# Two attention batches instead of one ahead of the layer, on the layer's own PSUM banks and buffers, and a planner that counts changes of the array's shape

## The chip, the cores and the metric

The kernel runs on one core of a Trainium2 chip. The metric is the device time of one execution in microseconds (us), the median of several runs. The core has five engines, each with its own queue that runs in order: TensorE (PE in the profile, with PEld for its weight loads), VectorE (DVE), ScalarE (ACT), GpSimd (POOL) and SyncE (SP). SP does no arithmetic here: it issues every DMA of the kernel.

## The reference

A linear attention over 8 batches of 8 heads, 576 tokens and head size 64, followed by a two-matrix layer with a Gelu over all 4608 tokens:

```python
def phi(x):                                   # (8, 8, 576, 64) -> (8, 8, 576, 256)
    proj = np.einsum('bhsd,df->bhsf', x, w_phi)
    proj = proj - np.max(np.abs(proj), axis=-1, keepdims=True)
    return np.concatenate([np.exp(proj), np.exp(-proj)], axis=-1)

q_p, k_p = phi(q), phi(k)
kv  = np.einsum('bhsf,bhsd->bhfd', k_p, v)
z   = np.sum(k_p, axis=2)
num = np.einsum('bhsf,bhfd->bhsd', q_p, kv)
den = np.einsum('bhsf,bhf->bhs', q_p, z)[..., None] + 1e-06
x   = (num / den).transpose(0, 2, 1, 3).reshape(4608, 512)
h   = x @ w_in                                # (4608, 2048)
g   = 0.5 * h * (1.0 + erf(h / sqrt(2)))
out = g @ w_out                               # (4608, 512)
```

## The kernel before, in words

Attention is done batch by batch. `k_quad(b, g)` takes four of a batch's heads. It loads `kt` and `vt`, and in five units it projects keys on PE (tile `pk`), takes the largest absolute value (`mx`) and subtracts it on DVE, takes two exponentials on ACT (`ek`), and sums keys times values on PE into `kv`, which ACT copies to `kvn`. `q_pair(b, p)` takes two heads and handles the tokens in two halves of 288: it projects queries on PE (`pq`), ACT copies them to `pc`, POOL takes the largest absolute value over the partitions (`mb`), DVE subtracts it from `pc`, ACT takes two exponentials (`ef`), and PE multiplies them with `kvn` (`pn`). ACT copies the result to `xo`, and it goes to device memory as `x_d`. The first two batches (`ND = 2`) get the denominator as a 65th row of `pn`. For the other six DVE weights `ef` (`un`) and POOL sums it over the partitions (`db`). `quotients` turns a half batch's denominators into reciprocals `r_d`.

The layer (`block(j, ...)`) runs over 18 blocks of 256 tokens. A block loads `xr` and `rb` (numerators and reciprocals), and DVE makes `xh` and `xl`, the high and low part of their product. Eight steps follow, each with 24 matmuls into `ph`, a Gelu on ACT (`gh`, and `ph` in place), a subtraction on DVE (`gl`), and 12 matmuls into `po`. The weights come as raw 64-bit words: `split_weight` turns each of 32 pieces into a high and a low float with two ACT and five DVE instructions (tiles `wt_` and `w_`). A piece may start 3.996 us after the one before.

Nothing runs in the order in which it is written. Each step is recorded with an engine, a cost, a rank and its buffers, and a planner (`Plan.order`) walks through a model of the engines and writes each engine's program in the order of its modelled starts. Among the steps of an engine that could start within 0.02 us of the earliest, the one with the lowest rank goes first. The chip then runs these fixed orders, each step waiting for what it needs, so a step that comes late holds up all that stands behind it on its engine.

PSUM is shared out as `pp` (two banks, for `pk` and `pq`), `kv`, `pn`, `ph` (two single banks) and `po` (two banks). Only batch 0 goes ahead of the layer: it does both its `k_quad`s first, then all four pairs of one half, then of the other, and its `pk` tiles take turns on `pp` and `po`. The other seven batches are spread over the layer by their ranks.

Of the kernel before, what the change touches and what calls it, by code (L numbers as in the profile page):

```python
# [58 lines left out]
class Plan:
# [191 lines left out]
def fused_kernel(ctx: ExitStack, tc: tile.TileContext, qT, kT, va, w_st, w_in, w_out, out):  # L251
# [48 lines left out]
    def split_weight(src, nm, rank):  # L300
# [8 lines left out]
        op("act", act(512), lambda: nc.scalar.activation(t().bitcast(F32), high().bitcast(F32), AF.Abs), r=[raw], w=[t], **k)  # L309
# [36 lines left out]

    def k_quad(b, g, kvs, rank):
# [18 lines left out]
        for u, (p, cs) in enumerate(units):  # L366
            n = len(cs)
            mx = sb["mx"]([P, 2, n], F32, f"mx_{nm}_{u}")
            e = [sb["ek"]([P, 2, n, NF], F32, f"ek_{nm}_{u}_{s}") for s in range(2)]
# [11 lines left out]
            for s in (1, 0):  # L381
                op("act", act(256 * n, True), lambda xs=xs, e=e, s=s: nc.scalar.activation(  # L382
                    e[s](), xs(), AF.Exp, scale=1.0 - 2.0 * s), r=[x], w=[e[s]], table="exp", **k())
# [24 lines left out]
    def q_pair(b, p, kvs, rank, halves=(0, 1)):  # L408
# [4 lines left out]
        for half in halves:  # L413
# [7 lines left out]
            op("pe", SW + PAIR_Q, lambda pq=pq, qt=qt: [
                mm(pq()[:, j, :HS], lhsT=wst()[64 * j : 64 * j + 64], rhs=qt()[64 * j : 64 * j + 64], start=True, stop=True) for j in range(2)
            ], r=[qt, wst], w=[pq], also=[pc], **k(1))
            copy("act", act(2 * HS, True), pc, lambda pq=pq: pq()[:, :, :HS], [pq], [pc], **k(1))
# [231 lines left out]
```

## Time and profile before

| | |
|---|---|
| median of 3 runs | 1194.47 us (1192.34 to 1195.37) |
| the profiled execution | 1194.14 us, of which the span from first to last instruction is 1192.4 us |
| PE busy | 1131.1 us, 95% of the span |
| ACT, DVE, POOL busy | 602.6, 496.4 and 318.6 us |
| mean granted TensorE clock | 0.977 of full |

The profiled execution is 0.3 us below the median of the runs, and its span lies 1.7 us below its own time. PE's share of busy time is an average over three stages that look different: a head before the layer's first matmul, a stage in which attention and layer share PE, and an end with the layer alone. The views of single stages say more than the page's totals. One matmul of 32-bit floats in the program counts as two in the trace, so that 1280 `kv` matmuls of the program are the 2560 of the page.

### The profile page before, as it was taken

What the parts mean: (1) busy time and instruction counts of PE and PEld (TensorE: products, weight loads), DVE (VectorE), ACT (ScalarE), POOL (GpSimd) and SP (SyncE); (2) the same over time, 40 slices, a digit from 0 to 9 for tenths busy, and PEclk for the clock granted to TensorE, in tenths of its full rate; (3) what the DMA queues carried; (4) which work ended last, traced back from release to release, by engine and by line L of the source; (5) the groups of instructions that cost most, each with busy time, mean ns of one, the idle gap of its engine ahead of it and who ended that gap; (6) DMA issues with size and microseconds to landing.
All of it is one profiled execution on the core that took longest, in us unless ns stands there. A gap on an engine that the chain in (4) does not pass through costs nothing.

```text
span 1192.4 us, 21799 instructions
## 1 busy us (share of the span) xinstructions
PE 1131.1 (95%) x9096; PEld 926.4 (78%) x9096; DVE 496.4 (42%) x807; ACT 602.6 (51%) x973; POOL 318.6 (27%) x116
## 2 busy tenths in 40 slices
PE   5669999989999999998989999999999999999998
PEld 3437688667887878776868787787899899899897
DVE  5888962375444444445253534434221121121110
ACT  4667866746557656665665654767222122122121
POOL 3110200376355353534152625435200000000000
PEclk8798999999999999998989999999999999999999
DMA  7467511242222222222113131201121111010000
GB/s 253 164 189 225 151 64 51 57 130 63 88 75 76 67 74 73 63 68 73 52 40 97 32 108 28 71 24 57 30 54 32 23 53 33 21 37 18 1 18 18
DMA packets 73939, 84.92 MB, mean 71 GB/s; under 512 B 23968, under 2 KB 60992, under 8 KB 73840
## 3 DMA queue, kind: packets, MB, share of 16 engines
q1 hardware_dynamic: 73840, 83.52, 23.6%
q8 instruction: 71, 1.16, 0.4%
q14 instruction: 28, 0.23, 0.1%
HBM read 64.32 MB, written 19.17 MB: 70 GB/s over the span
## 4 chain that ended last, share of the span: by engine, by line
PE 75%; DVE 8%; DMA 6%; ACT 4%; POOL 3%; issue 2%; SPq 1%; ACTq 0%; DVEq 0%; POOLq 0%
PE po L270 31%; PE ph L270 29%; PE kv L270 6%; PE pn L270 4%; POOL db L460 3%; PE pq L270 3%; PE pk L270 3%; DMA rb<-r_d 1%; DVE un L454 1%; DVE mx L378 1%; ACT ek L382 1%; DMA dc<-d_d 1%; DVE un L457 1%; DMA xr<-x_d 1%; DMA raw_i<-in_w_in_dram 1%
## 5 line engine op out<-in xcount | busy, mean ns | idle before, releaser
L270 PE MATMUL ph<-xh,w_i 128*128 128x256 f32 x2304 | 439.1, 284 | 0.0
L270 PEld LDWEIGHTS ph<-xh,w_i 128*128 128x128 f32 x2304 | 364.8, 190 | 18.2 <-issue 10.4
L270 PE MATMUL po<-w_o,gh 128*128 128x512 f32 x1152 | 370.6, 403 | 1.4 <-ACT ob L288 1.3
L270 PE MATMUL ph<-xl,w_i 128*128 128x256 f32 x1152 | 323.8, 281 | 0.0
L294 DVE TENSOR_TENSOR gl<-ph,gh 128x512 fp32r<-128x512 f32 x144 | 99.2, 689 | 378.5 <-ACT ph L548 366.8
L270 PEld LDWEIGHTS po<-w_o,gh 128*128 128x128 f32 x1152 | 209.5, 190 | 55.1 <-issue 10.9
L270 PE MATMUL po<-w_o,gl 128*128 128x512 f32 x576 | 230.7, 401 | 14.0 <-DVE gl L294 14.0
L425 POOL PARTITION_ALL_REDUCE mb<-pc x64 | 142.8, 2231 | 371.6 <-ACT pc L288 284.4
L270 PEld LDWEIGHTS ph<-xl,w_i 128*128 128x128 f32 x1152 | 218.4, 190 | 3.4
L460 POOL PARTITION_ALL_REDUCE db<-un x48 | 177.3, 3694 | 156.1 <-DVE un L457 152.3
L547 ACT ACTIVATE gh<-ph 128x512 fp32r<-128x512 f32 x144 | 86.1, 598 | 258.3 <-PE ph L270 257.7
L270 PEld LDWEIGHTS po<-w_o,gl 128*128 128x128 f32 x576 | 109.5, 190 | 44.0 <-DVE gl L294 18.8
L270 PEld LDWEIGHTS kv<-vt,ek 128*64 128x64 f32 (+1 forms) x2560 | 89.4, 145 | 44.0 <-ACT ek L382 18.1
L270 PE MATMUL kv<-vt,ek 128*64 128x65 f32 (+1 forms) x2560 | 102.0, 233 | 16.0 <-ACT ek L382 13.4
L270 PE MATMUL pn<-ef,kvn 128*64 128x288 f32 (+1 forms) x512 | 98.4, 426 | 14.1 <-ACT xo L288 11.8
L382 ACT ACTIVATE ek<-pk 128x512 f32<-128x512 f32 (+1 forms) x160 | 80.7, 549 | 54.1 <-DVE pk L294 53.7
L431 ACT ACTIVATE ef<-pc 128x576 f32<-128x576 f32 x128 | 81.0, 678 | 37.2 <-DVE pc L294 36.7
L547 ACT ACT_TABLE_LOAD x60 | 77.0, 1283 | 29.7 <-PE ph L270 28.9
L378 DVE TENSOR_REDUCE mx<-pk 128x4 f32<-128x512 f32 (+1 forms) x80 | 50.5, 632 | 97.4 <-PE pk L270 97.4
L548 ACT ACTIVATE ph<-ph 128x512 f32<-128x512 f32 x144 | 85.3, 593 | 0.0
L294 DVE TENSOR_TENSOR pc<-pc,mb 128x576 f32<-128x576 f32 x64 | 50.1, 783 | 77.1 <-POOL mb L425 77.1
L270 PEld LDWEIGHTS pn<-ef,kvn 128*64 128x64 f32 (+1 forms) x512 | 39.7, 138 | 51.2 <-ACT xo L288 20.4
(41 smaller groups left out, 718.9 us busy)
## 6 DMA issues: line engine op xcount, KB each, us to landing
vt<-in_va_dram SPq DMA_DIRECT2D x16, 585.0 KB
qt<-in_qT_dram SPq DMA_DIRECT2D x64, 144.0 KB
kt<-in_kT_dram SPq DMA_DIRECT2D x16, 576.0 KB
out_dram<-ob SPq DMA_DIRECT2D x36, 256.0 KB
raw_i<-in_w_in_dram SPq DMA_DIRECT2D x16, 512.0 KB
raw_o<-in_w_out_dram SPq DMA_DIRECT2D x16, 512.0 KB
x_d<-xo SPq DMA_DIRECT2D x48, 144.0 KB
x_d<-xo SPq DMA_DIRECT2D x32, 72.0 KB
```

The lines of the kernel that those rows point to most:

```text
L270: return tc.keep_in_program_order(nc.tensor.matmul(*a, **kw))
L294: op(eng, cost, lambda: e.tensor_tensor(out=dst(), in0=a(), in1=b(), op=o), r=r, w=w, **kw)
L378: op("dve", dve(256 * n, True), lambda xs=xs, mx=mx: nc.vector.tensor_reduce(out=mx(), in_=xs(), axis=AX.X, op=ALU.max, apply_absolute_val ...
L382: op("act", act(256 * n, True), lambda xs=xs, e=e, s=s: nc.scalar.activation(e[s](), xs(), AF.Exp, scale=1.0 - 2.0 * s), r=[x], w=[e[s]], ...
L425: op("pool", 2.2, lambda mb=mb, pc=pc: nc.gpsimd.partition_all_reduce(mb(), pc(), P, bass_isa.ReduceOp.absmax), r=[pc], w=[mb], **k(1))
L431: op("act", act(2 * HS), lambda ef=ef, pc=pc, s=s: nc.scalar.activation(ef()[:, s], pc(), AF.Exp, scale=1.0 - 2.0 * s), r=[pc], w=[ef], ta ...
L454: op("dve", dve(HS, fast=True) + 0.06, lambda un=un, ef=ef, one=one, j=j: nc.vector.tensor_scalar(out=un()[:, j], in0=ef()[:, 0, j], scala ...
L457: op("dve", dve(HS) + 0.06, lambda un=un, ef=ef, one=one, j=j: nc.vector.scalar_tensor_tensor(out=un()[:, j], in0=ef()[:, 1, j], scalar=on ...
L460: op("pool", 3.7, lambda db=db, un=un: nc.gpsimd.partition_all_reduce(db(), un(), P, bass_isa.ReduceOp.add), r=[un], w=[db], **k())
L547: op("act", act(2 * TB, True), lambda gh=gh, ph=ph: nc.scalar.activation(gh(), ph(), AF.Gelu), r=[ph], w=[gh], table="gelu", rank=URGE + rk)
L548: op("act", act(2 * TB, True), lambda ph=ph: nc.scalar.activation(ph(), ph(), AF.Gelu), r=[ph], w=[ph], table="gelu", rank=URGE + rk)
```

## The change

It has two parts.

The first part takes batches 0 and 1 ahead of the layer (`EB = 2`). Both go pair by pair (a `k_quad`, then the two pairs that need it), as the later batches do. Their `pk` tiles take turns on `pp` and `po` from unit to unit, their `pq` tiles go into the two `ph` banks (so that ACT copies each in two pieces), and every second unit's `ek` goes into an `xh` or `xl` buffer. No step of the layer may be planned before 90 us (`TF`).

The second part changes the planner. Steps on PE get a kind, `f` for the layer, `k`, `q`, `v`, `n`, `d` for attention. The fixed surcharge `SW` of 0.18 us on some steps is gone; in its place a step costs more where its kind uses the array in another shape than the step before. And where the last step on PE was the layer's, attention steps are held back until 2.5 us of them are together (`LUMP`) or one has waited 3 us (`LINGER`). A few modelled ACT costs rise by 0.016 to 0.04 us. Those are numbers of the model and change the order alone.

```diff
 class Plan:
+    BEHIND = {"f": 0.0, "k": 0.0, "q": 0.0, "v": 0.095, "n": 0.05, "d": 0.09}
+    BEFORE = {"f": 0.0, "k": 0.09, "q": 0.09, "v": 0.09, "n": 0.09, "d": 0.09}
+    SHAPE = {"f": 0, "k": 1, "q": 1, "v": 2, "n": 2, "d": 3}
...
                 lim = max(t0, clock[e]) + 0.02
+                hold = 0.0
+                if e == "pe" and last[0] == "f":
+                    t_of = {id(o): max(o.ready, first.setdefault(o.n, t)) for t, o in opts}
+                    there = [o for t, o in opts if t <= lim and o.kind != "f"]
+                    if sum(o.cost for o in there) < LUMP and all(lim - t_of[id(o)] < LINGER for o in there):
+                        hold = 4000.0
...
+                        if o.kind != "f":
+                            k += hold
...
+            if o.eng == "pe":
+                if self.SHAPE[last[0]] != self.SHAPE[o.kind]:
+                    cost += self.BEHIND[last[0]] + self.BEFORE[o.kind]
+                last[0] = o.kind
...
     def k_quad(b, g, kvs, rank):
...
-            e = [sb["ek"]([P, 2, n, NF], F32, f"ek_{nm}_{u}_{s}") for s in range(2)]
-            x = ps[EARLY_PK[u % 2] if b == 0 else "pp"]([P, 2, 512], F32, f"pk_{nm}_{u}")
+            x = ps[EARLY_PK[turn[0] % len(EARLY_PK)] if b < EB else "pp"]([P, 2, 512], F32, f"pk_{nm}_{u}")
+            if b < EB and EARLY_E[turn[0] % len(EARLY_E)] != "ek":
+                both = sb[EARLY_E[turn[0] % len(EARLY_E)]]([P, 2, 2, n, NF], F32, f"ek_{nm}_{u}")
+                e = [both, both]
+                es = [lambda both=both, s=s: both()[:, s] for s in range(2)]
+            else:
+                e = [sb["ek"]([P, 2, n, NF], F32, f"ek_{nm}_{u}_{s}") for s in range(2)]
+                es = [lambda s=s, e=e: e[s]() for s in range(2)]
+            turn[0] += 1
...
     def q_pair(b, p, kvs, rank, halves=(0, 1)):
...
-            pq = ps["pp"]([P, 2, 512], F32, f"pq_{nm}")
+            if b < EB:
+                pqs = [ps["ph"]([P, HS], F32, f"pq_{nm}_{j}") for j in range(2)]
+                of = [lambda t=t: t() for t in pqs]
+            else:
+                pqs = [ps["pp"]([P, 2, 512], F32, f"pq_{nm}")]
+                of = [lambda j=j, t=pqs[0]: t()[:, j, :HS] for j in range(2)]
...
     def attention(b, rank):
         kvs = {}
-        if b == 0:
+        if b == 0 and EB < 2:
...
     for b in range(1, B):
         plan.since = HOLD if b == 1 else 0.0
+        if b < EB:
+            plan.since = 0.0
+            attention(b, steps(-200.0 + EPACE * b, 0.01))
+            continue
...
-    plan.since = 0.0
+    plan.since = TF
     for j in range(NBLK):
...
+EARLY_E = ("ek", "xh", "ek", "xl")
+EB = 2
+EPACE = 20.0
+TF = 90.0
-SW = 0.18
+LUMP = 2.5
+LINGER = 3.0
```

What this does to the fixed orders shows at three places. In the rows below a name like `pn_1_3_1_1` is the tile `pn` of batch 1, pair 3, half 1, head 1, and the last number only tells buffers apart.

PE, the last rows ahead of the layer's first matmul (`ph_0_0`), before:

```order
L270 MATMUL pk_1_0_2_871<-wst_68,kt_1_0_479 128x128 x2
L270 MATMUL pn_0_3_1_1_876<-ef_0_3_1_811,kvn_0_1_1_645 65x288 x2
L270 MATMUL kv_1_0_0_741<-vt_1_0_481,ek_1_0_2_0_897 64x65 x2
L270 MATMUL kv_1_0_0_741<-vt_1_0_481,ek_1_0_2_1_894 64x65 x2
L270 MATMUL kv_1_0_0_741<-vt_1_0_481,ek_1_0_2_0_897 64x65 x2
L270 MATMUL kv_1_0_0_741<-vt_1_0_481,ek_1_0_2_1_894 64x65 x2
L270 MATMUL pk_1_0_3_910<-wst_68,kt_1_0_479 128x128 x4
```

and now:

```order
L287 MATMUL pn_1_3_0_1_1414<-ef_1_3_0_1369,kvn_1_1_1_1315 65x288 x2
L287 MATMUL kv_2_0_0_1399<-vt_2_0_984,ek_2_0_0_0_1392 64x65 x2
L287 MATMUL kv_2_0_0_1399<-vt_2_0_984,ek_2_0_0_1_1389 64x65 x2
L287 MATMUL kv_2_0_0_1399<-vt_2_0_984,ek_2_0_0_0_1392 64x65 x2
L287 MATMUL kv_2_0_0_1399<-vt_2_0_984,ek_2_0_0_1_1389 64x65 x2
L287 MATMUL pn_1_3_1_0_1435<-ef_1_3_1_1408,kvn_1_1_1_1315 65x288 x2
L287 MATMUL pk_2_0_1_1444<-wst_68,kt_2_0_908 128x128 x4
L287 MATMUL pn_1_3_1_1_1459<-ef_1_3_1_1408,kvn_1_1_1_1315 65x288 x2
L287 MATMUL ph_0_0_1471<-xh_0_1431,w_i0_0_257 128x256
```

Batch 1 was in its first `k_quad` there, and now it has given its last `pn`. Counted over all rows ahead of `ph_0_0`, PE's program holds 16 `pq`, 50 `pk`, 208 `kv` and 32 `pn` matmuls before, and 32, 80, 336 and 64 now.

DVE, the rows that end with `xr_0`, the first of the three instructions that make block 0's input, before:

```order
L314 SCALAR_TENSOR_TENSOR wt_i0_2_802<-raw_i0_2_698,wt_i0_2_802 128x512
L294 TENSOR_TENSOR w_o7_827<-wt_o7_738,w_o7_827 128x512
L316 SCALAR_TENSOR_TENSOR wt_i0_2_802<-raw_i0_2_698,wt_i0_2_802 128x512
L310 TENSOR_SCALAR wt_i1_2_851<-wt_i1_2_851 128x512
L312 TENSOR_SCALAR wt_i1_2_851<-wt_i1_2_851 128x512
L294 TENSOR_TENSOR w_i0_2_853<-wt_i0_2_802,w_i0_2_853 128x512
L294 TENSOR_TENSOR xr_0_342<-xr_0_342,rb_0_806 128x1024
```

and now:

```order
L311 TENSOR_TENSOR w_i3_2_1365<-wt_i3_2_1317,w_i3_2_1365 128x512
L404 TENSOR_REDUCE mx_2_0_0_1374<-pk_2_0_0_1358 128x4
L327 TENSOR_SCALAR wt_o8_1356<-wt_o8_1356 128x512
L311 TENSOR_TENSOR pk_2_0_0_1358<-pk_2_0_0_1358,mx_2_0_0_1374 128x2x256
L327 TENSOR_SCALAR wt_o8_1356<-wt_o8_1356 128x512
L311 TENSOR_TENSOR pc_1_3_1_1350<-pc_1_3_1_1350,mb_1_3_1_1371 128x576
L331 SCALAR_TENSOR_TENSOR wt_o8_1356<-raw_o8_1064,wt_o8_1356 128x512
L311 TENSOR_TENSOR xr_0_1214<-xr_0_1214,rb_0_1216 128x1024
```

Ahead of `xr_0` now stands batch 1's last `pc` too. In DVE's program 123 rows stood before `xr_0` and 167 do now. The added ones are 7 `mx` of 128x4 and 2 of 128x2, as many `pk`, 8 `pc`, the two `dc` instructions once more, and 3 `w_` (L294 before), 5 of L314 and L316, and 4 of L310 and L312.

DVE in the stage that attention and layer share, the first two halves of batch 5 (`un` is DVE's part of the denominator, which POOL's `db` must read before the next `un` may be written), before:

```order
L454 TENSOR_SCALAR un_5_0_0_5509<-ef_5_0_0_5477,kvn_5_0_0_5231 128x288 x2
L457 SCALAR_TENSOR_TENSOR un_5_0_0_5509<-ef_5_0_0_5477,kvn_5_0_0_5231,un_5_0_0_5509 128x288 x2
L454 TENSOR_SCALAR un_5_0_1_5564<-ef_5_0_1_5512,kvn_5_0_0_5231 128x288 x2
L457 SCALAR_TENSOR_TENSOR un_5_0_1_5564<-ef_5_0_1_5512,kvn_5_0_0_5231,un_5_0_1_5564 128x288 x2
L378 TENSOR_REDUCE mx_5_1_1_5594<-pk_5_1_1_5575 128x4
```

and now:

```order
L489 TENSOR_SCALAR un_5_0_0_5251<-ef_5_0_0_5202,kvn_5_0_0_4992 128x288 x2
L492 SCALAR_TENSOR_TENSOR un_5_0_0_5251<-ef_5_0_0_5202,kvn_5_0_0_4992,un_5_0_0_5251 128x288 x2
L311 TENSOR_TENSOR gl_5_0_5278<-ph_5_0_5155,gh_5_0_5249 128x512
L311 TENSOR_TENSOR gl_5_1_5292<-ph_5_1_5233,gh_5_1_5280 128x512
L489 TENSOR_SCALAR un_5_0_1_5311<-ef_5_0_1_5283,kvn_5_0_0_4992 128x288 x2
```

Two of the layer's `gl` now stand between the two `un`, where nothing stood before. Of the 47 places where one `un` follows another half's, 6 had nothing between them before and 2 have nothing now; at most two instructions stood between them at 16 places before and at 16 now. Over the whole stage the shape of the array changes 377 times before and 310 times now.

More of the change, by code (lines that the diff above doesn't have):

```diff
@@ L55 @@
 class Op:
-    __slots__ = ("eng", "cost", "fn", "bufs", "rank", "table", "late", "deps", "users", "wait", "ready", "start", "end", "n", "names", "nbytes", "duty")
+    __slots__ = ("eng", "cost", "fn", "bufs", "rank", "table", "late", "deps", "users", "wait", "ready", "start", "end", "n", "names", "nbytes", "duty", "kind")
 class Plan:
@@ L73, in pool, with op @@
         return lambda shape, dt, name: Buf(self, tag, lambda: pool.tile(shape, dt, tag=tag, name=name, bufs=bufs))
-    def op(self, eng, cost, fn, r=(), w=(), also=(), rank=0.0, table=None, late=0.0, kb=0, duty=1.0):
+    def op(self, eng, cost, fn, r=(), w=(), also=(), rank=0.0, table=None, late=0.0, kb=0, duty=1.0, kind="f"):
         o = Op()
         o.eng, o.cost, o.fn, o.rank, o.table, o.late, o.n = eng, cost, fn, rank, table, late, len(self.ops)
-        o.users, o.ready, o.nbytes, o.duty = [], self.since, kb, duty
+        o.users, o.ready, o.nbytes, o.duty, o.kind = [], self.since, kb, duty, kind
         deps = set()
@@ L137, in order @@
         clk = {"i": 0, "full": False, "busy": 0.0}
+        last, first = ["f"], {}
         def run(t, work, duty):
@@ L342, in fused_kernel @@
             for p in range(4)] for b in range(B)]
+    turn = [0]
     def k_quad(b, g, kvs, rank):
@@ L375, in proj @@
                            start=True, stop=True) for i, c in enumerate(cs) for j in range(2)]
-            op("pe", SW + n * PAIR_K, proj, r=[kt, wst], w=[x], also=[mx, *e], **k())
+            op("pe", n * PAIR_K, proj, r=[kt, wst], w=[x], also=[mx, *e], kind="k", **k())
             op("dve", dve(256 * n, True), lambda xs=xs, mx=mx: nc.vector.tensor_reduce(
@@ L391, in k_quad, with sums @@
                 for i, c in enumerate(cs):
-                    def sums(acc=acc, rs=rs, c=c, i=i, e=e, first=fresh and i == 0, last=last_u and i == n - 1):
+                    def sums(acc=acc, rs=rs, c=c, i=i, es=es, first=fresh and i == 0, last=last_u and i == n - 1):
                         ins = []
@@ L419, in q_pair @@
             mb = sb["mb"]([P, 2, HS], F32, f"mb_{nm}")
-            pq = ps["pp"]([P, 2, 512], F32, f"pq_{nm}")
[L421 to L424, printed above, removed]
+            if b < EB:
[4 more added lines that the diff above has]
+                of = [lambda j=j, t=pqs[0]: t()[:, j, :HS] for j in range(2)]
+            op("pe", PAIR_Q, lambda of=of, qt=qt: [
+                mm(of[j](), lhsT=wst()[64 * j : 64 * j + 64], rhs=qt()[64 * j : 64 * j + 64], start=True, stop=True) for j in range(2)
+            ], r=[qt, wst], w=pqs, also=[pc], kind="q", **k(1))
+            if b < EB:
+                for j in range(2):
+                    copy("act", act(HS, True), lambda pc=pc, j=j: pc()[:, j], of[j], [pqs[j]], [pc], **k(1))
+            else:
+                copy("act", act(2 * HS, True), pc, lambda t=pqs[0]: t()[:, :, :HS], pqs, [pc], **k(1))
             op("pool", 2.2, lambda mb=mb, pc=pc: nc.gpsimd.partition_all_reduce(
@@ L439, in q_pair @@
                         mm(pn()[: D + 1], lhsT=kvn()[:, 2 * s + j, :], rhs=ef()[:, s, j], start=s == 0, stop=s == 1) for s in range(2)
-                    ], r=[kvn, ef], w=[pn], **k())
+                    ], r=[kvn, ef], w=[pn], kind="d", **k())
                     xo = sb["xo"]([P, HS], F32, f"xo_{nm}_{j}")
```

19 lines of the change are left out of this document (10 added, 9 removed).

## Prediction

> **What bounds the kernel now.** I read the page's chain first (PE carries most of it), then busy time by stage, then PE's and DVE's groups in each stage. These stretches come from two answers of the view by stretches; the columns are length, busy time (and count) of PE, PEld, DVE, ACT and POOL, granted clock, DMA share and GB/s:
>
> ```profile
> PE 75%; DVE 8%; DMA 6%; ACT 4%; POOL 3%; issue 2%; SPq 1%; ACTq 0%; DVEq 0%; POOLq 0%
> ...
> 0.00:93.40 93.40, 61.35 (x570) 38.02 (x572) 72.33 (x122) 53.99 (x105) 18.60 (x12) 0.81 0.62 203
> 20.00:93.40 73.40, 49.32 (x502) 31.55 (x500) 64.36 (x108) 44.67 (x90) 13.67 (x6) 0.80 0.58 181
> 8.10:99.00 90.90, 60.08 (x613) 38.70 (x612) 77.36 (x131) 54.41 (x108) 18.41 (x8) 0.79 0.61 196
> ...
> 99.00:846.00 747.00, 723.61 (x6298) 576.14 (x6294) 358.68 (x596) 472.27 (x727) 299.43 (x104) 0.99 0.26 75
> 846.00:1192.40 346.40, 341.57 (x2182) 309.28 (x2182) 59.82 (x81) 74.42 (x138) 0.55 (x1) 1.00 0.10 27
> ```
>
> From 99 us on PE is the bound: 23.4 us idle in 747, and next to none in the end with the layer alone. Ahead of that it isn't: from 8.1 to 99 us PE idles for 30.8 us and runs at a clock of 0.79, while from 20 to 93.4 us DVE works 64.4 of 73.4 us. The border is the layer's first matmul, and just ahead of it the DVE chain that makes its input (start, length, instruction):
>
> ```profile
> 93.48 1.23 DVE L294 TENSOR_TENSOR xr<-xr,rb 128x1024 f32<-128x1024 f32 x1 [0.54 <-DMA rb<-r_d]
> 94.95 0.68 DVE L290 CAST xh<-xr 128x1024 fp32r<-128x1024 f32 x1
> ...
> 99.00 0.39 PE L270 MATMUL ph<-xh,w_i 128*128 128x256 f32 x1
> ```
>
> So the time is the head's length plus the PE work left behind it plus what PE loses there. The change moves PE work from behind the border to ahead of it, and the question is by how much the border moves back.
>
> **Work that leaves the PE-bound stage.** The groups of PE in the stretch 99 to 846 us (count, busy us, mean ns of one):
>
> ```profile
> L270 PE MATMUL kv<-vt,ek 128*64 128x65 f32 x1728 | 61.8, 224 | 1.6 <-ACT ek L382 1.6
> L270 PE MATMUL pn<-ef,kvn 128*64 128x288 f32 x384 | 57.3, 419 | 2.1 <-ACT ef L431 1.6 <-ACT xo L288 0.5
> L270 PE MATMUL pk<-wst,kt 64*128 64x128 f32 x476 | 44.3, 300 | 0.0
> L270 PE MATMUL pq<-qt,wst 64*128 64x288 f32 x224 | 42.3, 455 | 0.9 <-ACT ek L382 0.6 <-ACT pc L288 0.3
> L270 PE MATMUL pn<-ef,kvn 128*65 128x288 f32 x64 | 18.6, 413 | 2.2 <-ACT xo L288 2.2
> L270 PE MATMUL kv<-vt,ek 64*64 64x65 f32 x420 | 18.0, 224 | 1.6 <-ACT kvn L288 1.6
> ```
>
> The means overlap, so I price one by busy time over count. By the orders 128 `kv`, 30 `pk`, 16 `pq` and 32 `pn` go ahead of the border, twice as many in the trace's counting: 256 `kv` at 79.8/2148 = 37 ns, 9.5 us; 60 `pk` at 93 ns, 5.6 us; 32 `pq` at 189 ns, 6.0 us; and the whole row of 64 `pn` with 65 rows, 18.6 us. Together 39.7 us. This holds the price of changing the array's shape as those matmuls paid it.
>
> The lumps save a little more. One change costs what stands between two starts beyond the usual:
>
> ```profile
> 419.16 0.73 PE L270 MATMUL po<-w_o,gh 128*128 128x512 f32 x2
> 419.73 0.39 PE L270 MATMUL po<-w_o,gl 128*128 128x512 f32 x1
> 419.96 0.64 PE L270 MATMUL po<-w_o,gh 128*128 128x512 f32 x2
> 420.44 0.39 PE L270 MATMUL po<-w_o,gl 128*128 128x512 f32 x1
> 420.75 0.76 PE L270 MATMUL pq<-qt,wst 64*128 64x288 f32 x4
> ```
>
> The first pair of `po`, after attention, took 0.57 us to the next start, the second 0.48: 0.09 for coming back. From `gl` on to `pq` took 0.31, on to `po` 0.23: 0.08 for going over. Of the 377 changes the moved work would take along between 16% (its share of attention's busy time) and 12% (its share of `kv`), which leaves 315 to 332. There are 310, so the lumps spare 5 to 22 changes at 0.085 us: about 1 us. The stage behind the border loses **41 us** of work.
>
> **How far the border moves back.** DVE's groups ahead of `xr_0`, in the stretch 0 to 93.4 us:
>
> ```profile
> L314 DVE SCALAR_TENSOR_TENSOR wt_i<-raw_i,wt_i 128x512 uint32<-128x512 uint32 x9 | 7.1, 794 | 0.2
> L294 DVE TENSOR_TENSOR pk<-pk,mx 128x512 f32<-128x512 f32 x10 | 6.8, 686 | 0.0
> L378 DVE TENSOR_REDUCE mx<-pk 128x4 f32<-128x512 f32 x10 | 6.7, 679 | 0.2 <-PE pk L270 0.2
> L294 DVE TENSOR_TENSOR w_o<-wt_o,w_o 128x512 fp32r<-128x512 f32 x8 | 6.2, 769 | 2.7 <-ACT w_o L288 2.7
> L294 DVE TENSOR_TENSOR pc<-pc,mb 128x576 f32<-128x576 f32 x8 | 6.0, 747 | 10.4 <-POOL mb L425 10.4
> L310 DVE TENSOR_SCALAR wt_i<-wt_i 128x512 f32<-128x512 f32 x10 | 5.0, 495 | 1.5 <-ACT wt_i L309 1.3
> L294 DVE TENSOR_TENSOR pk<-pk,mx 128x256 f32<-128x256 f32 x2 | 0.8, 420 | 0.0
> ```
>
> By these durations the added rows are 14 `mx` and `pk` of the larger form, 9.6 us; 4 of the smaller, 1.7; 8 `pc`, 6.0; 3 `w_`, 2.3; 5 of L314's kind, 4.0; 4 of L310's, 2.0; two `dc`, 0.4: 26 us. Durations overlap here (the 17 groups of this stretch sum to 79.1 us against 72.3 busy), so busy time grows by 26 x 0.914 = 23.8 us. With the idle time as it is, the border goes back by **24 us**. PE asks for about as much. PE's groups in the stretch 0 to 99 us:
>
> ```profile
> L270 PE MATMUL pn<-ef,kvn 128*65 128x288 f32 x64 | 22.5, 481 | 9.8 <-ACT xo L288 9.1 <-ACT kvn L288 0.7
> L270 PE MATMUL kv<-vt,ek 128*64 128x65 f32 x320 | 16.6, 279 | 6.6 <-ACT ek L382 6.6
> L270 PE MATMUL pk<-wst,kt 64*128 64x128 f32 x100 | 9.8, 331 | 2.9 <-ACT pc L288 2.9
> L270 PE MATMUL pq<-qt,wst 64*128 64x288 f32 x32 | 7.2, 532 | 5.3 <-ACT ek L382 4.6 <-ACT pc L288 0.7
> L270 PE MATMUL kv<-vt,ek 64*64 64x65 f32 x96 | 5.9, 287 | 6.1 <-ACT ek L382 5.2 <-ACT kvn L288 0.9
> ```
>
> At this stage's rates (352, 98, 225 and 54 ns) the moved matmuls take 22.5 + 5.9 + 7.2 + 13.8 = 49.4 us, more than their 39.7 behind the border since the clock is lower here. The head would then end at 8.1 + 60.1 + 49.4 = 117.6 us without any idle time of PE, 19 us later. PE's idle time, all of it waits for ACT, must therefore nearly go, or the clock must rise. The free banks and buffers serve that: with `pq` off `pp` and twice the `ek` buffers, two chains of `pk` and one of `pq` run side by side. ACT stands at 54 of 93.4 us and has room. The ends: DVE's 9.0 us of idle time after 20 us all filled, 24 - 9 = 15 us; PE's idle time of 30.8 us all kept, 19 + 31 = 50 us. I take 24, nearer to DVE's row because DVE is the fuller engine now.
>
> In the Trainium skill ("SBUF — State Buffer", section "Who interferes with whom") a DVE copy, cast or tensor_scalar in a two-port mode and a GpSimd instruction shut each other out for a whole instruction. The cast above at 0.68 us and the one at 615.63 below, 3.01 us long, agree. Twice as many `mb` now fall into the head, and by that rule each of the 8 new ones could hold such an instruction for its own length.
>
> **What PE loses behind the border.** 23.4 us of idle time, and a clock of 0.99 over 747 us, about 7 us more: 30 us. The largest losses all have one form, here at 542 and 615 us:
>
> ```profile
> 536.69 2.31 DVE L454 TENSOR_SCALAR un<-ef,kvn 128x288 f32<-128x288 f32 x2 [3.72 <-POOL db L460]
> 547.34 0.79 PE L270 MATMUL po<-w_o,gl 128*128 128x512 f32 x1 [4.81 <-DVE gl L294]
> ...
> 615.20 4.19 POOL L460 PARTITION_ALL_REDUCE db<-un  x1 [1.83 <-DVE un L457]
> ...
> 615.63 3.01 DVE L290 CAST xh<-xr 128x1024 fp32r<-128x1024 f32 x1
> 620.56 0.79 PE L270 MATMUL po<-w_o,gl 128*128 128x512 f32 x1 [5.09 <-DVE gl L294]
> ```
>
> An `un` stands behind another with nothing between, DVE waits for POOL, the layer's `gl` is late behind it, and PE waits 5 us and then runs about 2.5 us' worth slower. Two such places are left of six. I take one stall of that size off, 7 us, with all 30 us kept as one end and, if both go and the small ones with them, 18 us off as the other. Holding attention steps back costs nothing by itself, since PE does the layer's work meanwhile; behind a held step wait only `mx`, `ek` and `kvn`, which have slack in a stage where DVE is busy 359 of 747 us.
>
> **The sum.** 1194.1 us (the profiled execution, 0.3 us below the median) + 24 - 41 - 7 = **1170 us**. From no change (1194.5) a measurement here tells 0.3%, some 3.6 us.
>
> **The rivals.**
> - The head fills and the shared stage runs clean: border +15, losses -18: 1194 + 15 - 41 - 18 = 1150 us. For it: two chains in place of one, a clock that rises with PE's load (0.79 at 66% busy, 1.00 at 99%). Against: DVE has never been above 96% busy. The skill's clock gate ("TensorE: Matmul & The Clock Gate", "What's actually happening") opens the clock after one busy window of some 3.4 us, which the two clocks bear out. Chance 0.20.
> - **Slower**: PE's queue in the head stays as full of waits as it is. PE runs its rows in order, and one `pn` bank still makes each `pn` wait for an `xo` (9.1 us of waits for 64). All 30.8 us of idle time kept, the border goes back by 50 us: 1203 us without the 7 us, 1196 with them. It decides from a border past 140 us. Against it: those waits are for banks and buffers that the change doubles. Chance 0.10.
> - New late `gl` behind the border: at 16 places at most two instructions stand between two `un`, as before. Each further stall costs 7.5 us; two more than now eat 15 us: 1192. Chance 0.08.
> - The shut-out port: 8 more `mb` of 2.2 us, one blocked instruction each, 14 us beyond what the rows' means hold: border +38, 1184 us. In the head the tensor_scalars take 0.50 us against 0.42 undisturbed, 3 us in all for 8 `mb`, which speaks against. Chance 0.07.
> - Nothing changes, because the layer's first block waits for its weights instead: 20 of 32 pieces are done at `xr_0`, and 12 more at 3.3 us of DVE make 40 us, against 66 us that block 0 and its attention take on PE. Chance 0.05, 1192 us.
>
> **How the numbers follow.** The forecast as worked out, 1160 to 1182 us, has a chance of 0.50. Range: the first rival lies at its low end and the port at its high end, and what lies above is left out: 1152 to 1189 us. Faster by more than 0.3%: 0.50 + 0.20 + 0.07, and 0.06 of the second and third rivals: 0.83. Within: 0.05 and another 0.05 of these two. Slower: 0.07.
>
> **What would show it.** Right: first `ph` at 115 to 130 us, PE's clock ahead of it near 0.9, DVE above 88% busy there, some 41 us less of attention matmuls behind it, fewer waits of `po` for `gl` above 4 us. Wrong: a first `ph` past 140 us with PE waiting for `xo` and `ek`, or more than 30 us lost behind it.

## The result, and the profile after

The changed kernel takes 1155.55 us (median, 1152.61 to 1158.21), the kernel before 1194.85 in the same comparison: a ratio of 0.9675, with a 95% interval of 0.9642 to 0.9707. The profiled execution is 1153.51 us, its span 1151.7. First the chain that ended last, by engine, then the same kind of stretches as in the prediction: ahead of the border (twice), the shared stage, the layer alone.

```profile
PE 85%; DVE 7%; DMA 3%; ACT 2%; issue 1%; SPq 1%; POOL 0%; ACTq 0%; DVEq 0%; POOLq 0%
```

```profile
8.10:123.90 115.80, 92.33 (x1027) 57.43 (x1025) 103.96 (x173) 86.67 (x189) 36.87 (x16) 0.93 0.70 221
20.00:123.90 103.90, 84.87 (x917) 51.98 (x917) 96.29 (x159) 78.51 (x171) 30.98 (x14) 0.92 0.68 209
123.90:763.20 639.30, 629.88 (x5598) 507.67 (x5597) 311.67 (x544) 416.90 (x635) 281.13 (x96) 1.00 0.25 72
763.20:1151.70 388.50, 383.55 (x2470) 346.36 (x2468) 67.37 (x90) 83.79 (x154) 0.00 (x0) 1.00 0.10 28
```

The border stands at 123.9 us (99.0 before). Ahead of it PE idles 115.8 - 92.3 = 23.5 us (30.8 before) although the head is 25 us longer, and its clock is 0.93 (0.79). Behind it the rest takes 1027.8 us instead of 1093.4: 65.6 us less. PE's groups in the shared stage, to be read against the prediction's rows of the stretch 99 to 846:

```profile
L287 PE MATMUL pn<-ef,kvn 128*64 128x288 f32 x384 | 57.2, 419 | 0.9 <-ACT xo L305 0.9
L287 PE MATMUL kv<-vt,ek 128*64 128x65 f32 x1504 | 53.8, 224 | 2.1 <-ACT ek L408 2.1
L287 PE MATMUL pk<-wst,kt 64*128 64x128 f32 x416 | 39.3, 303 | 0.3 <-ACT pc L305 0.3
L287 PE MATMUL pq<-qt,wst 64*128 64x288 f32 x192 | 36.3, 455 | 0.2 <-ACT ek L408 0.2
L287 PE MATMUL kv<-vt,ek 64*64 64x65 f32 x384 | 16.4, 224 | 1.8 <-ACT kvn L305 1.1 <-ACT ek L408 0.7
L287 PE MATMUL pn<-ef,kvn 128*65 128x288 f32 x2 | 0.6, 406 | 0.0
```

They sum to 203.6 us; before, the six groups summed to 242.3. So 38.7 us of attention left the stage, and with 1 us for the spared changes of shape (forecast, not measured alone) about 40. The other 26 us are not attention work. The waits behind the border, before (99 to 839 us) and after (123.9 to 763.2); the columns are the sum, the number and the longest:

```profile
DVE un L454 <- POOL db L460: 30.8, 9, 3.8
PE po L270 <- DVE gl L294: 13.5, 5, 5.1
```

```profile
DVE un L489 <- POOL db L495: 16.0, 11, 3.8
PE po L287 <- DVE gl L311: 4.2, 3, 2.3
```

The two stalls of 5 us are gone, and so is most of the half rate that went with them. Leaving out the last microseconds of the program, the granted clock is at half in these stretches behind the border, three before and one after (same columns as above):

```profile
255.90:259.30 3.40, 3.40 (x9) 2.61 (x8) 0.85 (x2) 2.23 (x4) 3.40 (x1) 0.50 0.00 0
546.10:552.90 6.80, 5.56 (x16) 4.59 (x17) 2.45 (x4) 1.05 (x3) 0.07 (x1) 0.50 0.22 58
617.70:624.50 6.80, 3.94 (x9) 3.14 (x10) 3.81 (x6) 1.11 (x3) 1.69 (x1) 0.50 0.24 62
```

```profile
178.50:181.90 3.40, 3.40 (x14) 2.34 (x13) 2.97 (x6) 1.79 (x3) 1.63 (x1) 0.51 0.50 145
```

That is 17.0 us before and 3.4 after. PE worked for 12.9 and 3.4 us of them, so half rate cost about 6.5 us before and 1.7 after, 4.8 us less. PE's idle time behind the border fell from 28.2 to 14.4 us.

### The profile page after: what moved, and what is told of

Same layout as the page of the kernel before. It is cut to its first block, busy times and chain, and to the rows that moved or that the text cites. A ratio compares the mean times of both kernels' runs of the same rounds, so it can differ in the third digit from the quotient of the medians.

```text
span 1151.7 us, 21761 instructions
## 1 busy us (share of the span) xinstructions
PE 1111.6 (97%) x9096; PEld 914.0 (79%) x9096; DVE 483.5 (42%) x807; ACT 588.9 (51%) x979; POOL 318.2 (28%) x116
## 3 DMA queue, kind: packets, MB, share of 16 engines
q1 hardware_dynamic: 73840, 83.52, 24.3%
## 4 chain that ended last, share of the span: by engine, by line
PE 85%; DVE 7%; DMA 3%; ACT 2%; issue 1%; SPq 1%; POOL 0%; ACTq 0%; DVEq 0%; POOLq 0%
PE po L287 34%; PE ph L287 34%; PE kv L287 6%; PE pn L287 5%; PE pk L287 3%; PE pq L287 3%; DMA dc<-d_d 1%; DVE mx L404 1%; DVE pk L311 1%; DMA vt<-in_va_dram 1%; ACT ek L408 1%; DVE wt_o L331 1%; PE spin L287 1%; DMA x_d<-xo 1%; DVE w_i L311 0%
## 5 line engine op out<-in xcount | busy, mean ns | idle before, releaser
L287 PE MATMUL ph<-xh,w_i 128*128 128x256 f32 x2304 | 429.3, 282 | 0.0
L287 PEld LDWEIGHTS ph<-xh,w_i 128*128 128x128 f32 x2304 | 359.7, 188 | 13.5 <-issue 5.4
L287 PE MATMUL po<-w_o,gh 128*128 128x512 f32 x1152 | 366.9, 400 | 0.0
L287 PE MATMUL po<-w_o,gl 128*128 128x512 f32 x576 | 227.8, 395 | 4.2 <-DVE gl L311 4.2
L287 PEld LDWEIGHTS kv<-vt,ek 128*64 128x64 f32 (+1 forms) x2560 | 86.3, 141 | 41.6 <-ACT ek L408 18.0
L287 PE MATMUL pn<-ef,kvn 128*64 128x288 f32 (+1 forms) x512 | 98.8, 427 | 13.2 <-ACT xo L305 13.1
L287 PE MATMUL kv<-vt,ek 128*64 128x65 f32 (+1 forms) x2560 | 98.4, 229 | 13.3 <-ACT ek L408 11.7
L466 ACT ACTIVATE ef<-pc 128x576 f32<-128x576 f32 x128 | 83.1, 684 | 24.0 <-DVE pc L311 23.5
L287 PEld LDWEIGHTS pn<-ef,kvn 128*64 128x64 f32 (+1 forms) x512 | 39.3, 138 | 45.4 <-ACT xo L305 17.1
```

What stands on the lines that cost most here:

```text
L287: return tc.keep_in_program_order(nc.tensor.matmul(*a, **kw))
L466: op("act", act(2 * HS), lambda ef=ef, pc=pc, s=s: nc.scalar.activation(ef()[:, s], pc(), AF.Exp, scale=1.0 - 2.0 * s), r=[pc], w=[ef], ta ...
```

## The experiments

Each was compared with the kernel before on the same chip. "Border" is the start of the first layer `ph`; PE's idle time is told ahead of it (from 8.1 us) and behind it.

| kernel | median us | ratio and interval | border | idle ahead | idle behind |
|---|---|---|---|---|---|
| before | 1194.85 | 1 | 99.0 | 30.8 | 28.2 |
| the change | 1155.55 | 0.9675 [0.9642, 0.9707] | 123.9 | 23.5 | 14.4 |
| planner_alone | 1184.88 | 0.9921 [0.9905, 0.9936] | 92.6 | 27.2 | 24.1 |
| head_old_planner | 1184.63 | 0.9915 [0.9899, 0.9932] | 125.7 | 26.8 | 30.2 |
| no_lumps | 1173.63 | 0.9828 [0.9811, 0.9845] | 122.4 | 24.9 | 26.0 |
| smaller_lumps | 1156.58 | 0.9691 [0.9668, 0.9714] | 123.3 | 23.1 | 13.9 |
| bigger_lumps | 1163.49 | 0.9752 [0.9731, 0.9773] | 121.6 | 21.9 | 24.3 |
| one_ahead_late | 1186.02 | 0.9933 [0.9911, 0.9955] | 116.2 | 40.9 | 13.8 |
| pq_on_pp | 1171.10 | 0.9813 [0.9784, 0.9841] | 139.4 | 34.9 | 8.8 |
| no_x_buffers | 1157.17 | 0.9689 [0.9661, 0.9717] | 125.1 | 22.6 | 13.6 |
| early_loads | 1154.22 | 0.9671 [0.9653, 0.969] | 112.1 | 22.8 | 18.0 |
| three_ahead_nd3 | 1155.93 | 0.968 [0.9656, 0.9705] | 164.1 | 30.8 | 7.9 |
| lighter_split | 1142.50 | 0.9563 [0.9548, 0.9578] | 118.9 | 19.5 | 10.6 |
| sub_on_pool | 1282.46 | 1.0747 [1.0725, 1.077] | 235.8 | 110.0 | 22.8 |

**The two parts, each alone.** The planner with one batch ahead, and the banks and buffers of before:

```diff
-            x = ps[EARLY_PK[turn[0] % len(EARLY_PK)] if b < EB else "pp"]([P, 2, 512], F32, f"pk_{nm}_{u}")
+            x = ps[EARLY_PK[u % 2] if b < EB else "pp"]([P, 2, 512], F32, f"pk_{nm}_{u}")
...
-            if b < EB:
+            if b < 0:
                 pqs = [ps["ph"]([P, HS], F32, f"pq_{nm}_{j}") for j in range(2)]
...
-EARLY_E = ("ek", "xh", "ek", "xl")
-EB = 2
-TF = 90.0
+EARLY_E = ("ek",)
+EB = 1
+TF = 0.0
```

> The new planner (prices for the array's shape, lumps) with one batch ahead of the layer, on the banks and buffers of before. Theory A: the clean stage behind the border is the planner's doing, and the head's trade is a second, separate gain; then PE loses some 10 us behind the border instead of 30 and the time is about 1172 us (1165 to 1180), with the first ph near 99 us. Theory B: the stage is clean because less attention is left in it; then the planner alone gives nothing: 1190 to 1196 us, 25 us or more lost.

The two batches ahead, under the planner of before (the modelled ACT costs go back too):

```diff
-    BEHIND = {"f": 0.0, "k": 0.0, "q": 0.0, "v": 0.095, "n": 0.05, "d": 0.09}
-    BEFORE = {"f": 0.0, "k": 0.09, "q": 0.09, "v": 0.09, "n": 0.09, "d": 0.09}
+    BEHIND = dict.fromkeys("fkqvnd", 0.0)
+    BEFORE = dict.fromkeys("fkqvnd", 0.0)
...
-            op("pe", n * PAIR_K, proj, r=[kt, wst], w=[x], also=[mx, *e], kind="k", **k())
+            op("pe", SW + n * PAIR_K, proj, r=[kt, wst], w=[x], also=[mx, *e], kind="k", **k())
...
-LUMP = 2.5
+LUMP = 0.0
+SW = 0.18
```

> Two batches ahead on the layer's banks and buffers, but the planner of before: fixed surcharge, no price for the shape, no lumps. Theory A: the head's trade alone, 41 us of work gone from behind the border against 25 us of a longer head: about 1177 us (1170 to 1184), PE losing 25 to 30 us behind the border, some of it in waits of po for gl of 4 us and more. Theory B: about 1158 us, under 12 us lost.

Either part brings 10 us, both together 39. planner_alone lies between the ranges of its two theories, and head_old_planner 0.6 us above theory A's. The stretches ahead of the border, of the shared stage and of the layer alone, and then PE's largest wait in the shared stage (sum, number, longest), first of planner_alone, then of head_old_planner:

```profile
8.10:92.60 84.50, 57.33 (x573) 36.52 (x569) 72.50 (x124) 52.83 (x104) 18.73 (x8) 0.80 0.63 203
92.60:848.30 755.70, 736.02 (x6408) 588.65 (x6409) 361.43 (x604) 485.32 (x745) 297.79 (x104) 0.99 0.26 75
848.30:1182.50 334.20, 329.80 (x2110) 298.61 (x2108) 58.14 (x80) 71.63 (x132) 1.05 (x1) 1.00 0.10 28
```

```profile
PE po L287 <- DVE gl L311: 5.0, 8, 1.4
```

```profile
8.10:125.70 117.60, 90.83 (x1061) 56.75 (x1057) 108.01 (x178) 88.89 (x193) 36.88 (x16) 0.94 0.70 219
125.70:784.30 658.60, 633.10 (x5508) 506.51 (x5507) 324.81 (x533) 414.03 (x628) 276.05 (x95) 0.98 0.24 69
784.30:1183.10 398.80, 394.08 (x2524) 356.57 (x2522) 70.40 (x97) 86.75 (x159) 3.59 (x1) 1.00 0.11 29
```

```profile
PE po L287 <- DVE gl L311: 19.2, 10, 5.1
```

The old planner fills the head as well (PE 90.8 us busy there), but its shared stage gets worse: 25.5 us idle, half rate for 23.9 us, and 19.2 us of waits for `gl` where before had 13.5. The new planner alone clears the late part, with 1.8 us of PE's idle time between 350 us and the last attention against 13.6 before, but idles 16.5 us between 100 and 350 us against 9.8.

**The late start alone.** One batch ahead under the new planner, but the layer held back as in the change (planner_alone with `TF = 90.0`):

> The new planner, one batch planned ahead of the layer and the banks and buffers of before, but the layer held back to TF = 90 as in the changed kernel: 166 DVE instructions stand ahead of the first xr (changed kernel 167, planner alone 122), 240 kv matmuls ahead of the first ph (336 and 192). Both theories put the first ph at about 118 us (planner alone 92.6, the changed kernel 123.9) and take 14 us of work out of the stage behind it (48 of the 144 kv matmuls that were worth 41). Theory A, the steady stage became clean because the layer starts late, when the weights' split and the start of batch 1 no longer overlap it: the stage loses no more than the changed kernel's, which is 13 us less than with the planner alone, so 1090 - 14 - 13 = 1063 behind the border and 1183 in all. Theory B, it became clean because one batch less is left to be placed in it: the losses stay those of the planner alone, 1076 behind the border and 1196 in all.

The stretches ahead of the border, of the shared stage and of the layer alone:

```profile
8.10:116.20 108.10, 67.16 (x707) 42.99 (x705) 98.03 (x171) 67.25 (x130) 23.51 (x10) 0.82 0.65 208
116.20:814.40 698.20, 689.15 (x6062) 552.10 (x6061) 322.65 (x550) 461.08 (x701) 292.93 (x102) 0.99 0.24 71
814.40:1182.50 368.10, 363.35 (x2326) 329.00 (x2324) 63.68 (x87) 79.25 (x146) 0.00 (x0) 1.00 0.11 30
```

Behind the border 1066.3 us, near theory A's 1063. The work that moved was oversized in both theories: by the prediction's prices for each matmul it is 4 `pq`, 12 `pk`, 48 `kv` and 2 `pn` more in the program, 8.5 us and not 14. So of the 23.6 us saved behind the border 8.5 are work, 10.3 are idle time, and half rate is at most 4.5 (8.1 instead of 17.1 us of it): with the new planner a layer that starts later meets a cleaner stage. The border paid for all of it, 23.6 us, and the time stayed. From here to the change the border moves by 7.7 us only, while 12 `pq`, 22 `pk`, 96 `kv` and 30 `pn` (33 us by those prices) move ahead of it and the time behind it gets 38.5 us shorter: PE's idle time ahead falls from 40.9 to 23.5 us, and its clock there rises from 0.82 to 0.93. The second batch fills time that the late start had left empty.

**Which of the banks and buffers count.** The queries back on `pp`, then the exponentials back on `ek`:

```diff
-            if b < EB:
+            if b < 0:
                 pqs = [ps["ph"]([P, HS], F32, f"pq_{nm}_{j}") for j in range(2)]
```

> The changed kernel with the queries' projections of the early batches back on the pp banks, as one two-bank tile with one ScalarE copy, the layer's ph banks unused in the head; all else as in the change. Theory A, VectorE and SyncE's late loads set the border: first ph within 3 us of 123.9, and 1153 to 1160 us (two ScalarE copies of 288 become one of 576, which saves ScalarE some 0.2 us 16 times in the head, off the path). Theory B, the head lives on banks: pk and pq wait for each other on pp, the first ph comes 6 us later or more, and 1162 or more.

```diff
-EARLY_E = ("ek", "xh", "ek", "xl")
+EARLY_E = ("ek",)
```

> The changed kernel with the exponentials of both early batches on their own ek buffers again, none on the layer's xh and xl; all else as in the change. 165 DVE instructions ahead of the first xr (167), 62 pn ahead (64). Theory A, VectorE and SyncE's late loads set the border: first ph within 2 us of 123.9, and 1154 to 1159 us. Theory B, the head lives on buffers: pk waits for ek, the first ph comes 6 us later or more, and 1162 or more.

```profile
8.10:139.40 131.30, 96.39 (x1013) 59.17 (x1011) 113.20 (x189) 87.87 (x174) 36.89 (x16) 0.84 0.65 202
139.40:779.50 640.10, 636.03 (x5610) 512.00 (x5609) 297.65 (x528) 417.63 (x635) 277.84 (x96) 1.00 0.24 71
```

```profile
PE kv L287 <- ACT ek L408: 13.8, 6, 4.4
...
PE pk L287 <- ACT pc L305: 4.5, 4, 1.6
```

```profile
129.29 1.21 DVE L311 TENSOR_TENSOR xl<-xr,xh 128x1024 fp32r<-128x1024 f32 x1
...
138.57 1.19 PE L287 MATMUL pn<-ef,kvn 128*65 128x288 f32 x4 [1.20 <-ACT xo L305]
```

The rows are pq_on_pp's stretches ahead of the border and of the shared stage, its waits ahead of the border, and the end of its head. In pq_on_pp PE waits ahead of the border for `pc`, the copy that frees `pp` (4.5 us, none of it for `pk` in the change), and for `ek` (13.8 us against 8.9). The layer's input is ready at 130.5 us, and PE is still at attention, with waits, until the border at 139.4. The border goes back by 15.5 us and the time by about as much, as theory B said, whereas the `x` buffers make no difference that can be measured. It is the `ph` banks that carry the second batch.

**How far the head's VectorE work decides.** In lighter_split, one DVE instruction for each weight piece is left out, so the weights' low bits are missing:

```diff
-        op("dve", dve(512), lambda: v.scalar_tensor_tensor(
-            out=t(), in0=low(), scalar=29, in1=t(), op0=ALU.logical_shift_right, op1=ALU.bitwise_or), r=[raw, t], w=[t], **k)
+        op("dve", dve(512), lambda: [], r=[raw, t], w=[t], **k)
```

> The changed kernel with one of the five DVE instructions of each weight piece left out (the one that shifts in the low word's bits), all else in the same order. Some 21 of them stand ahead of xr_0, about 0.73 us each. If DVE bounds the head: the first ph at 110 to 114 us instead of 124 and the time 10 to 13 us lower, 1142 to 1147 us. If PE's own queue (waits for ACT) bounds it: first ph at 120 to 124 us, 1152 to 1156 us.

Ahead of the border, and the shared stage:

```profile
8.10:118.90 110.80, 91.28 (x1025) 57.22 (x1025) 91.69 (x152) 86.41 (x189) 36.01 (x16) 0.92 0.73 231
118.90:752.90 634.00, 628.34 (x5598) 506.68 (x5597) 304.15 (x533) 416.66 (x635) 282.21 (x96) 1.00 0.25 73
```

DVE is busy 12.3 us less ahead of the border (91.69 for 103.96), and the border moved by 5.0 us. So DVE does not set it alone: 118.9 lies in neither theory's range. The time is the one that the DVE theory gave, but only half of it was won ahead of the border: of the 10.3 us between the profiled executions 5.3 lie behind it, where PE idles 3.8 us less and the 3.4 us of half rate are gone. What else is there shows in the head's last rows in the changed kernel (start, length, instruction):

```profile
114.80 0.42 SPq L552 DMA_DIRECT2D xr<-x_d  x1
...
118.87 1.23 DVE L311 TENSOR_TENSOR xr<-xr,rb 128x1024 f32<-128x1024 f32 x1 [1.17 <-DMA xr<-x_d]
...
121.56 1.22 DVE L311 TENSOR_TENSOR xl<-xr,xh 128x1024 fp32r<-128x1024 f32 x1
...
123.05 1.19 PE L287 MATMUL pn<-ef,kvn 128*65 128x288 f32 x4
```

DVE waits for a load that SP issued only 4 us earlier. The layer's input is ready at 122.8 us, and PE's own queue holds a last `pn` step right ahead of the layer's first matmul at 123.9. early_loads lets SP issue the first block's loads earlier:

```diff
+        if j == 0:
+            plan.since = TL
...
+        plan.since = TF
         tt("dve", dve(NCC * TB), xr, xr, rb, ALU.mult, [xr, rb], [xr], rank=rank(0) - 4)
...
+TL = 72.0
```

> The changed kernel with the loads of the layer's first block planned from 72 on instead of 90, so that SyncE issues them ahead of the head's last stores; all else as in the change. 143 DVE instructions ahead of the first xr (changed kernel 167), 320 kv matmuls and 52 pn ahead of the first ph (336 and 64), so 4.6 us of attention work go back behind the border (16 of the 144 kv matmuls that were worth 41). Theory A, the late load and the instructions ahead of xr set the border: 24 instructions fewer at the second batch's price, 24.9 us for 45, bring it from 123.9 to about 111, and the time to 1147. Theory B, the last attention pieces on TensorE and the load were late together: the first ph moves by 3 us at most, and the work that goes back is paid in full, 1156 to 1161.

The border came 11.8 us earlier, as theory A said, and the time did not move, as theory B said. What stands behind it took 13.6 us more. The work that went back, 2 `pq`, 4 `pk`, 16 `kv` and 12 `pn`, makes 9.7 us at the prediction's prices, not 4.6, because a `pn` costs far more than a `kv`; the idle time grew by 3.6.

**Once more of the same.**

```diff
-EB = 2
+EB = 3
-TF = 90.0
+TF = 130.0
-ND = 2
+ND = 3
```

> The changed kernel with a third batch planned ahead of the layer (EB = 3, TF = 130, and a third set of the pairs' rotating buffers). 230 DVE instructions ahead of the first xr (167), 480 kv matmuls ahead of the first ph (336), 266 shape changes behind it (310). One batch more takes 41 us of work out of the stage, as the second did. Theory A, the trade can be repeated: the border goes back by (230 - 167) instructions at the second batch's price, 24.9 us for 45, so 35 us, to 159; behind it 1028 - 41 - 2 = 985, in all 1146. Theory B, the second batch only filled TensorE's idle time in the head (30.8 us, 23.5 now) and little is left to fill, so the third costs in front all it saves behind: border 165 or later, 1155 or more.

Ahead of the border, and the shared stage:

```profile
8.10:164.10 156.00, 125.23 (x1455) 79.05 (x1452) 143.64 (x237) 120.19 (x265) 52.33 (x23) 0.95 0.66 209
164.10:701.60 537.50, 533.97 (x4734) 429.79 (x4733) 242.12 (x430) 348.73 (x531) 235.85 (x81) 0.99 0.23 67
```

The time is theory B's, and the border within 1 us of it: it goes back by 40.2 us, the rest gets shorter by 35.5, and the time stays. The head had 23.5 us of PE's idle time left, and with the third batch it has more, not less. But the run changes two things. `ND = 3` is no set of buffers, as the expectation has it: it gives the third batch its denominator as a 65th row of `pn` on PE, in place of `un` on DVE and `db` on POOL. PE's `pn` rows sum to 108.0 us over the program for 98.8 in the change, and DVE is busy 467.3 us for 483.5. A third batch with `ND = 2` was not run, so how much of the cost in front is these 9 us of work is not shown.

**The hold.** Left out, halved, doubled:

```diff
-LUMP = 2.5
+LUMP = 0.0
```

> The changed kernel with the shape's prices but without lumps (attention steps are not held back). In its DVE order 7 places have nothing between two un, and 14 at most one instruction, against 2 and 4. If the lumps make the stage clean: 1163 to 1175 us, with waits of po for gl of several us. If the prices do, or nothing in the planner: 1154 to 1160 us. The 16 further changes of shape alone would cost 1.4 us.

```diff
-LUMP = 2.5
-LINGER = 3.0
+LUMP = 1.3
+LINGER = 1.5
```

> The changed kernel with about half the hold: LUMP 1.3 and LINGER 1.5 instead of 2.5 and 3.0. Behind the border 302 changes of array shape (changed kernel 310, without any hold 326); of two heads' un multiplications on VectorE 2 stand with at most one instruction between them and 7 with at most two (changed kernel 4 and 16, without the hold 14 with at most one). Theory A, the hold pays because it keeps VectorE's attention instructions apart, so that gl is not late: this kernel loses as little as the changed one, 1150 to 1158 us. Theory B, it pays because TensorE's attention work comes in long pieces: half the hold brings half of its 18 us, 1161 to 1168.

```diff
-LUMP = 2.5
-LINGER = 3.0
+LUMP = 5.0
+LINGER = 6.0
```

> The changed kernel with twice the hold: LUMP 5.0 and LINGER 6.0. Behind the border 295 changes of array shape (changed kernel 310), 15 pairs of un multiplications on VectorE with at most one instruction between them (4 in the changed kernel, 14 without the hold). Theory A, what counts is that VectorE's attention instructions stand apart: the waits of po for gl are back at 10 or more places (3 in the changed kernel, 12 without the hold), and 1163 to 1173 us. Theory B, what counts is the length of the pieces and the fewer changes: 1152 to 1157 us.

PE's largest waits behind the border, of no_lumps and of bigger_lumps:

```profile
PE po L287 <- DVE gl L311: 12.4, 12, 1.6
PE kv L287 <- ACT kvn L305: 4.0, 7, 1.4
```

```profile
PE kv L287 <- ACT ek L408: 6.6, 5, 4.3
PE po L287 <- DVE gl L311: 5.3, 5, 3.0
PE pn L287 <- ACT xo L305: 4.6, 1, 4.6
```

The hold is worth 18 us, of which 16 spared changes of shape make 1.4 at the prediction's price. Without it PE waits for `gl` at 12 places and idles 11.6 us more behind the border; the rest of the 18 us is not resolved. Half the hold does as much as the whole, so the gain does not grow with the length of the pieces between 1.3 and 2.5 us, as theory B had it. Twice the hold loses 8 us, but theory A's reason for that failed: with 15 close pairs of `un` PE waits for `gl` at 5 places, not 10, and the loss comes from attention's own results, since PE waits 4.3 us for `ek` and 4.6 us for `xo` at one place each. So the number of close `un` in the order does not tell the stalls. Why the hold keeps `gl` in time is not settled by these runs.

**Moving DVE's work to GpSimd.** The last step of each weight's split on POOL, with nothing left out:

```diff
-        tt("dve", dve(512), lambda: w()[:, 1, :], lambda: t().bitcast(F32), lambda: hi().bitcast(F32), ALU.subtract, [t, w], [w], **k)
+        tt("pool", 1.2, lambda: w()[:, 1, :], lambda: t().bitcast(F32), lambda: hi().bitcast(F32), ALU.subtract, [t, w], [w], **k)
```

> The changed kernel with the last step of each weight piece's split (w's low half = piece minus high half, 128x512) on GpSimd instead of VectorE, its cost planned as 1.2 us; nothing is left out. 141 DVE instructions ahead of the first xr (changed kernel 167), the same 80 pk and 336 kv matmuls ahead of the first ph. Theory A, VectorE's instructions in the head and the weights' pace bind, as the kernel with one instruction per piece left out showed (13 us for 21 instructions ahead of the first xr): 1142 to 1149 us. Theory B, the work only changes its place: GpSimd delays the sums and the fast forms of VectorE by as much as VectorE is spared, 1153 us or more.

Theory A missed by 133 us, and theory B's open bound holds the time without explaining it. POOL's groups, and four of its rows in order of time (the bracket is the idle time before one):

```profile
L495 POOL PARTITION_ALL_REDUCE db<-un x48 | 178.1, 3710 | 117.7 <-DVE un L492 114.3 <-DMA d_d<-db 3.4
L460 POOL PARTITION_ALL_REDUCE mb<-pc x64 | 140.2, 2190 | 292.6 <-ACT pc L305 203.9 <-issue 56.9 <-DVE pc L311 21.4
L311 POOL TENSOR_TENSOR w_i<-wt_i,w_i 128x512 fp32r<-128x512 f32 x16 | 21.5, 1349 | 76.3 <-issue 43.7 <-ACT w_i L305 25.4 <-DMA x_d<-xo 7.2
L311 POOL TENSOR_TENSOR w_o<-wt_o,w_o 128x512 fp32r<-128x512 f32 x16 | 20.7, 1297 | 57.2 <-ACT w_o L305 29.3 <-issue 27.9
```

```profile
64.24 2.34 POOL L460 PARTITION_ALL_REDUCE mb<-pc  x1 [0.97 <-DVE pc L311]
73.71 1.25 POOL L311 TENSOR_TENSOR w_o<-wt_o,w_o 128x512 fp32r<-128x512 f32 x1 [7.13 <-issue]
80.75 2.15 POOL L460 PARTITION_ALL_REDUCE mb<-pc  x1 [5.79 <-issue]
89.57 1.25 POOL L311 TENSOR_TENSOR w_o<-wt_o,w_o 128x512 fp32r<-128x512 f32 x1 [6.66 <-issue]
```

The subtraction takes 1.3 us, about as planned. But at all 22 changes from one kind of instruction to the other POOL stands idle for 5.7 to 7.9 us. At 19 of them, 128.5 us in all, nothing in the profile is waited for; the other three are put down to a semaphore that came within the gap. No two of the same kind have such a gap without a wait. The trace also holds instructions that the views leave out: a pair of MODIFY_POOL_CONFIG ahead of each of the 22 changes and otherwise only at the program's start, where every other kernel here has its one pair. From the pair to the next instruction it takes 5.4 to 7.7 us. The `mb` chains and the weights stand behind these gaps, and the border at 235.8.

## Why the prediction was right, and where it was off

The direction and the range held, and of the three steps two came out near their size; the time came out 14 us below the forecast, because the third did not.

- **Work that leaves the stage**, forecast 41 us: the rows show 38.7, and about 40 with the changes of shape. Right.
- **The border**, forecast +24, measured +24.9. The size was right, the reason only in part, and that it came so close is luck. The rows named as added ahead of `xr_0` are 40, while the programs differ by 44: the traces show 7 more of L314 and L316 together and 6 more of L310 and L312, not 5 and 4. With them the sum is 28.6 us, or 26 of busy time. DVE's busy time ahead of the border did grow by 26.6 us (77.4 to 104.0), and its idle time fell by 1.7, which the forecast had left as it was. DVE's sum was not the cause alone, either: by it lighter_split's border would come 12.3 us earlier, and it came 5.0; and that of pq_on_pp, with 173 DVE rows ahead of `xr_0` for 167, came 15.5 later. The held start (`TF`), the banks, SP's load and PE's queue come due together with DVE. On PE the clock rose, as one of the two ways out that the prediction named: the moved matmuls were priced at 49 us there, and PE's busy time ahead of the border grew by 32.3. (The prediction names 17 groups in the busy sum of 79.1 us; they are 18. Its 0.42 us for an undisturbed tensor_scalar stood without a row.)
- **What PE loses behind the border** is the term that failed: forecast -7, with -18 as the low end, measured 65.6 - 41 = 24.6 us. Of these 13.9 are idle time and 4.8 are half rate. About 6 are left, and in the layer alone the same matmuls run a little faster, here the largest group there, before (900 to 1180 us) and after (900 to 1140):

```profile
L270 PE MATMUL ph<-xh,w_i 128*128 128x256 f32 x800 | 146.4, 281 | 0.0
```

```profile
L287 PE MATMUL ph<-xh,w_i 128*128 128x256 f32 x698 | 125.5, 278 | 0.0
```

  One block alone takes 44.80 us before and 44.55 after, which would make 4.5 us over 18 blocks. This pace goes with the program: it is 44.55 in no_lumps, smaller_lumps, early_loads, lighter_split and three_ahead_nd3 too, 44.80 in planner_alone and one_ahead_late, and 44.9 in head_old_planner, no_x_buffers and pq_on_pp. Its cause is open. The step went wrong by pricing two stalls one by one. It took the planner's part as 1 us of spared changes plus one stall, and the late border as a pure cost. The runs show that the hold alone is worth 18 us, and that a later border under the new planner takes 10.3 us of idle time and up to 4.5 of half rate out of the stage behind (one_ahead_late against planner_alone), while under the old planner the stage got worse. Each part alone brought 10 us, and the other 20 came only with both; by the paces above some 6 of them (an estimate, taken over all 18 blocks) are the layer's pace. Why the stage runs clean with both was not separated further.
- **The rivals.** "The head fills and the shared stage runs clean" was half right: the stage, not the border. PE's queue full of waits did not come, though pq_on_pp shows how it would: on the old `pp` banks the border lies at 139.4. Waits of `po` for `gl` came three times, none above 2.3 us. The shut-out port would have put the border at 137; it stood at 123.9, and the 128x512 tensor_scalars ahead of `xr_0` took 0.515 us on average before and after, with twice as many `mb` beside them. The long cast that the prediction shows ended 0.75 us before the `db` beside it did, so those rows show a slow cast, and not for sure one that was shut out. The weights did not hold the first block by the 40 us that rival needed: no wait for a weight is among PE's waits in the shared stage, which sum to 9.5 us. And that the clock opens in windows of 3.4 us can't be read from two mean clocks; the stretches of half rate above, 3.4 and 6.8 us long, do fit it.

## What to carry to other kernels

Where one engine is the bound, count its idle time and its slow clock over the whole program: early_loads, three_ahead_nd3 and the change have their borders 52 us apart and take the same time. Work moved ahead of a border pays only as far as it fills time that is empty there; the third batch, with its dearer `pn`, no longer paid. Before a planner's change is priced by the stalls one can name, try it together with what it will meet, since each part alone showed a quarter of the gain here.

## What was not expected of the hardware

GpSimd lost 5.7 to 7.9 us at every one of the 22 changes between a tensor_tensor and a partition_all_reduce. The Trainium skill ("GPSIMD Engine Reference", section "2.1 Instruction dispatch") tells of about 6 us for loading a kernel's code at its first call, with no instruction in the profile. The size agrees, and a pair of MODIFY_POOL_CONFIG instructions stands at the start of each gap. But here the gap comes back at each change in both directions, not only at a first call: the gap ends 5.4 to 6.0 us after the pair at nine of the eleven changes to a partition_all_reduce, and 6.6 to 7.7 us after it at all eleven to a tensor_tensor. What goes on inside the gap the trace does not show.
